# Attention: when the value products of a head pair are issued, and which engine copies the transposed scores out of PSUM

## The chip, the cores and the metric
One core of a Trainium2 chip. A time is device microseconds (us) of one execution; the kernel before takes 1093.11 us, the median of three runs (1092.77 to 1093.15).

## The reference
Rotary attention, and behind it two feed-forward layers on its output:

```
q, k, v: 4 x 8 heads x 576 x 64
scores = (1/8) * rotate(q) @ rotate(k)^T;  scores -= max over the keys
attn   = exp(scores) / (sum + 1e-9);       out = attn @ v
x = out as 2304 tokens x 512
x = elu(x @ w_in) @ w_out          (512 -> 2048 -> 512)
x = h - tanh(h), h = x @ w_in2;  x @ w_out2
```

## The kernel before
Attention works through 16 pairs of heads. One pair is nine steps: four blocks of 128 queries for each of the two heads (items 0 to 7, the heads alternating) and one item, 8, with the last 64 queries of both. Lines 402 to 436 write the order of the instructions out by hand, step by step over all pairs (i = 9 x pair + item), so every engine takes its work in exactly this order. Step i issues:

- VectorE: the row maximum of item i (L241, tile nm).
- TensorE: the scores of item i+1 (L232, tile s). There are two PSUM buffers for s, so these scores can only be written when the exponential of item i-1 has read its buffer.
- ScalarE: the exponential of item i out of PSUM into tile a (L255), with the row sums.
- flush (L282): the copies (evacuations) out of PSUM of what step i-1 transposed. The tile aT takes 128x512 elements of each item, aTr 128x128 for each second item and for item 8. A running counter ev shares the copies out: two of five go to VectorE (L286), three of five to ScalarE (L288). They are 14 in a pair, so which copy falls to which engine repeats after five pairs. After them flush copies finished outputs o to xa on ScalarE (L293).
- VectorE adds 1e-9 and takes the reciprocal of the row sums for items that are complete (L268, L269), and GpSimd (POOL) scales a by it (L272).
- A piece of the next pair's rotation (GpSimd L148, VectorE L150 and L157, ScalarE L153; from it q and k are put in place by DMAs on SP's queue, L194 and L197), and in some steps a piece of a feed-forward weight's conversion (L74 to L92).
- TensorE: the transposes of item i-4 (four into pt, L312; for each second item one more into pr, L322, and for item 8 L316). There are three PSUM buffers for pt and pr.
- TensorE: the value products that are due (L345, tile o). They come in visits. A group of queries (items 0 to 3; items 4 to 7; item 8) has five chunks of keys; for each chunk there is one product for each head, which stands in the trace as two instructions. Here the stationary matrix is 128 x 64, where scores and transposes use 128 x 128 (the form column says 128*64 and 128*128).

PV_AT (L401) gives for each group and chunk how many steps after the group's last transpose it is issued. Before the change a pair p has four visits: at step 8 of pair p three chunks of the first group (12 instructions); at step 1 of pair p+1 its other two (8); at step 3 three chunks of the second group (12); at step 5 its other two and the last group (28). The visit at a distance of 1 step reads aT tiles whose copies stand in the flush of the same step, behind that step's exponential.

The first pair's scores come out of a shorter path. After attention the first feed-forward layer (L472, L529) and the second (L758, L723) follow.

Of the kernel before, what the change touches and what calls it, by code (L numbers as in the profile page):

```python
# [23 lines left out]
def attention_elu_tanhshrink(ctx: ExitStack, tc: tile.TileContext, qk, v, w1i, w1o, w2i, w2o, tab, out):  # L24
# [35 lines left out]
    def load_w(key, eng=nc.sync):  # L60
        l, kind, c = key
        t = fm[:, 1024 * (nraw[0] % 2):1024 * (nraw[0] % 2) + 1024]
        nraw[0] += 1
        eng.dma_start(out=t.bitcast(mybir.dt.int64), in_=w_src[l, kind][c])
        raw_t[key] = t
# [43 lines left out]
    with ExitStack() as actx:  # L109
# [20 lines left out]
        def load_qk(p, x):  # L130
            t = p2.tile([128, 2, S], F32, tag=f"t{x}", name=f"t{x}")
            nc.sync.dma_start(out=t, in_=qk[p, :, 2 * x:2 * x + 2, :])
            t_t[p, x] = t

        def load_v(p):
            t = v_t[p] = vt_t[p % 2]
            nc.sync.dma_start(out=t[:, 0:512], in_=v[p, :, 0:512])
            for h in range(2):
                sl = slice(64 * h, 64 * h + 64)
                nc.sync.dma_start(out=t[sl, 512 + 64 * h:576 + 64 * h], in_=v[p, sl, 512:576])  # L140
            nc.sync.dma_start(out=t[64:128, 640:704], in_=v[p, 0:64, 512:576])
# [25 lines left out]
        def rotate_first(x):  # L167
            t = t_t.pop((0, x))
            prod = ps_s.tile([128, 2, 512], F32, tag="s", name="prod")[:, :, 0:288]
            for i in range(2):  # L170
                yield
                nc.vector.scalar_tensor_tensor(
                    out=two(t[:, 1, :]) if i else prod, in0=two(t[:, i, :]), scalar=(1.0 if x else SCALE),
                    in1=two(tabs[:, i, :]), op0=ALU.mult, op1=ALU.mult,
                )
            yield
            if x:
                nc.vector.tensor_tensor(out=two(rk), in0=prod, in1=two(t[:, 1, :]), op=ALU.add)
            else:
                for h in range(2):  # L180
                    sl = slice(64 * h, 64 * h + 64)
                    nc.vector.tensor_tensor(
                        out=two(rq[:, h, :])[sl], in0=prod[sl], in1=two(t[:, 1, :])[sl], op=ALU.add
                    )
            yield
# [53 lines left out]
        def emit_max(i):  # L239
            nm = sm.tile([128, 1], F32, tag="nm", name="nm")  # L240
            nc.vector.tensor_reduce(out=nm, in_=s_t[i][:, :, 0:288], axis=AX.XY, op=ALU.max, negate=True)  # L241
            nm_t[i] = nm

        def emit_exp(i):
            p, u, h = items[i]
            s = s_t.pop(i)
            if h in (0, None):
                if u < 4:
                    a_t[p, u] = p3.tile([128, 2, S], F32, tag="a", name="a")
                else:  # L250
                    a_t[p, u] = p1.tile([128, 1, S], F32, tag="a2", name="a2")
                n_t[p, u] = sm.tile([128, 2], F32, tag="den", name="den")
            a = a_t[p, u][:, h or 0, :]
            den = n_t[p, u][:, (h or 0):(h or 0) + 1]
            nc.scalar.activation(  # L255
                out=a.rearrange("p (x c) -> p x c", x=2), in_=s[:, :, 0:288], func=AF.Exp,
                bias=nm_t.pop(i), scale=1.0, accum_out=den,
            )

        def emit_norm(i):  # L260
            p, u, h = items[i]
            if h == 0:
                return
            nh = 2 if h == 1 else 1
            den = n_t.pop((p, u))[:, 0:nh]
            r = sm.tile([128, 2], F32, tag="r", name="r")
            for x in range(nh):
                nc.vector.tensor_scalar_add(den[:, x:x + 1], den[:, x:x + 1], 1e-9)  # L268
            nc.vector.reciprocal(out=r[:, 0:nh], in_=den)  # L269
            for x in range(nh):  # L270
                a = a_t[p, u][:, x, :]
                nc.gpsimd.tensor_scalar(  # L272
                    out=a, in0=a, scalar1=r[:, x:x + 1], scalar2=1.0, op0=ALU.mult, op1=ALU.mult
                )

        ev = [0]
# [5 lines left out]
        def flush():  # L282
            for out_, in_ in late:
                ev[0] += 1
                if ev[0] % 5 in (1, 3):
                    nc.vector.tensor_copy(out_, in_)  # L286
                else:
                    nc.scalar.copy(out_, in_)  # L288
            late.clear()
            for p, grp, o, n in late_x:  # L290
                b, hp = divmod(p, 4)
                x0 = NTOK * hp + b * S + 256 * grp
                nc.scalar.copy(out=xa[:, x0:x0 + n], in_=o[:, 0:n])  # L293
            late_x.clear()
# [75 lines left out]
        with tc.manual_schedule():  # L370
            for x in range(2):
                t_t[0, x] = p2.tile([128, 2, S], F32, tag=f"t{x}", name=f"t{x}")
            for i in range(2):
                nc.sync.dma_start(out=t_t[0, 1][:, i, :], in_=qk[0, :, 2 + i, :])
                nc.sync.dma_start(out=tabs[:, i, :], in_=tab[:, i, :])
                nc.sync.dma_start(out=t_t[0, 0][:, i, :], in_=qk[0, :, i, :])
            load_qk(1, 1)
            load_qk(1, 0)
            nc.vector.memset(xa[:, 0:512], 0.0)
            nc.vector.memset(zero, 0.0)  # L380
            nc.gpsimd.memset(rq[64:128, 0, :], 0.0)
            nc.gpsimd.memset(rq[0:64, 1, :], 0.0)
            make_identity(nc, ident)
            warm = ps_t.tile([128, 512], F32, tag="pt", name="warm")
            for i in range(8):
                nc.tensor.matmul(out=warm, lhsT=xa[:, 0:128], rhs=xa[:, 0:512], start=True, stop=True)
            for i in range(2):
                nc.scalar.copy(out=qa_t[i][:, S:640], in_=zero)
                nc.scalar.copy(out=qb_t[i][:, 0:64], in_=zero)
                nc.gpsimd.memset(vt_t[i][64:128, 512:576], 0.0)  # L390
                nc.gpsimd.memset(vt_t[i][0:64, 576:704], 0.0)
            rot = [rotate_first(1), rotate_first(0)]
            for i in range(4):
                for r in rot:
                    next(r)
            n = len(items)
            pend = []
            nw = list(range(len(first_w)))[::-1]
            emit_s(0)
            load_v(0)  # L400
            PV_AT = ((1, 1, 1, 3, 3), (1, 1, 1, 3, 3), (2, 2, 2, 2, 2))  # L401
            for i in range(n + D + 1):
                p, r = divmod(i, NI)
                for f, *arg in sched.get(i, ()):
                    if f is not prep:
                        f(*arg)
                if i == 7 or i % (2 * NI) == 12:
                    load_w(first_w[nw.pop()]) if nw else None
                if i < n:
                    emit_max(i)  # L410
                if i + 1 < n:
                    emit_s(i + 1)
                if i < n:
                    emit_exp(i)
                flush()
                if 0 <= i - 1 < n:
                    emit_norm(i - 1)
                if p < NPAIR:
                    for f, *arg in sched.get(i, ()):
                        if f is prep:  # L420
                            f(*arg)
                    c = r if p == 1 else NI * (p % 2) + r - 3 if p else -1
                    if c >= 0 and c % 2 == 0 and c // 2 < NCV and p // 2 < len(first_w):
                        key = first_w[p // 2]
                        conv_w(key, c // 2, 512 * (p // 2 % 3))
                if 0 <= i - D < n:
                    emit_t(i - D)
                    pp, uu, hh = items[i - D]
                    if uu in (1, 3) and hh == 1 or uu == 4:
                        for c in range(5):  # L430
                            pend.append((i + PV_AT[uu // 2][c], pp, uu // 2, c))
                for x in [x for x in pend if x[0] <= i]:
                    emit_pv(*x[1:])
                    pend.remove(x)
                if n - 8 <= i < n and (i - n) % 2 == 0:
                    split_x(0, (i - n + 8) // 2)
            while pend:
                emit_pv(*pend.pop(0)[1:])
            flush()


# [519 lines left out]
```

## Time and profile before

| | |
|---|---|
| median of three runs | 1093.11 us |
| the profiled execution | 1093.27 us, of which the profile's span 1090.8 us |
| TensorE (PE) busy | 1066.9 us, 98% of the span |
| VectorE (DVE) busy | 753.3 us, 69% |
| ScalarE (ACT) busy | 723.1 us, 66% |
| GpSimd (POOL) busy | 696.5 us, 64% |
| TensorE clock granted | full throughout |

Attention takes the first 302 us of the span; pair p's visit at step 8 starts at about 47 us for pair 1 and 277 us for pair 14. PE's busy time counts overlapping instructions whole and is no measure of how well it is used; the order of the waits tells more. PEld are TensorE's weight loads, which run ahead of its products.

### The profile page before, as it was taken

How to read it: one execution, taken by the hardware profiler on the slowest of the kernel's cores; microseconds unless marked ns; L12 is line 12 of the kernel's file. 1: busy time of each engine (PE TensorE's matmuls, PEld its weight loads, DVE VectorE, ACT ScalarE, POOL GpSimd, SP SyncE). 2: the span in 40 equal slices, each digit the busy share in tenths (PEclk: the TensorE clock that was granted, in tenths of full speed). 3: DMA queues.
4: the chain of work that ended last, by engine and by line, in shares of the span. 5: the costliest groups of instructions: out<-in, count | busy, mean ns of one | idle time of the engine just before them, and what ended most of it. 6: DMA issues, size and time to landing. Idle time of an engine off the chain costs nothing.

```text
span 1090.8 us, 18762 instructions
## 1 busy us (share of the span) xinstructions
PE 1066.9 (98%) x6480; PEld 959.0 (88%) x6480; DVE 753.3 (69%) x1436; ACT 723.1 (66%) x1560; POOL 696.5 (64%) x653
## 2 busy tenths in 40 slices
PE   8999999999999999999999999999999999999998
PEld 4777777777799999999999999988998999889986
DVE  7898888888546456675675665376766667766674
ACT  3677677777668656555555555588777877878762
POOL 5887888887568755555555556566567555755552
PEclk9999999999999999999999999999999999999999
DMA  7878777776224344354344672265545664556531
GB/s 237 224 185 214 178 206 195 206 199 173 59 69 143 129 153 136 117 164 166 115 145 139 216 260 81 94 224 202 175 163 176 248 212 175 176 167 221 172 126 58
DMA packets 86590, 182.75 MB, mean 168 GB/s; under 512 B 11745, under 2 KB 47585, under 8 KB 86497
## 3 DMA queue, kind: packets, MB, share of 16 engines
q1 hardware_dynamic: 78720, 153.25, 44.7%
q10 hardware_dynamic: 7776, 28.32, 8.7%
q8 instruction: 51, 0.84, 0.3%
q14 instruction: 43, 0.34, 0.1%
HBM read 127.21 MB, written 27.79 MB: 142 GB/s over the span
## 4 chain that ended last, share of the span: by engine, by line
PE 76%; DVE 11%; POOL 4%; ACT 3%; DMA 3%; issue 2%; SPq 0%; ACTq 0%; DVEq 0%; POOLq 0%
PE y L529 18%; PE h L472 18%; PE yb L723 14%; PE hb L758 9%; PE o L345 6%; PE s L232 5%; PE cvb L758 3%; PE pt L312 3%; DVE nm L241 3%; DVE aT L286 1%; DVE fn L791 1%; DMA qb<-hl 1%; ACT a L255 1%; POOL blk L513 1%; DVE t L150 1%
## 5 line engine op out<-in xcount | busy, mean ns | idle before, releaser
L513 POOL TENSOR_TENSOR gt<-fn,gt 128x384 fp32r<-128x384 f32 x119 | 123.1, 1035 | 78.2 <-ACT gt L512 66.2
L272 POOL TENSOR_SCALAR a<-a,r 128x576 f32<-128x576 f32 x144 | 138.4, 973 | 48.2 <-DVE r L269 31.1
L255 ACT ACTIVATE a<-s,nm 128x576 f32<-128x576 f32 x144 | 107.0, 743 | 90.7 <-DVE nm L241 76.0
L723 PE MATMUL yb<-wb,blk 128*128 128x512 f32 x603 | 154.3, 392 | 0.4 <-POOL blk L513 0.4
L758 PE MATMUL hb<-blk,wa 128*128 128x384 f32 x720 | 139.9, 337 | 2.0 <-DVE fn L791 2.0
L758 PEld LDWEIGHTS hb<-blk,wa 128*128 128x128 f32 x720 | 127.1, 188 | 7.3 <-DVE fn L791 3.0
L723 PEld LDWEIGHTS yb<-wb,blk 128*128 128x128 f32 x603 | 112.5, 188 | 22.6 <-POOL blk L513 0.8
L480 ACT ACTIVATE fn<-h 128x384 f32<-128x384 f32 x96 | 47.3, 493 | 128.4 <-PE h L472 109.6
L241 DVE TENSOR_REDUCE nm<-s 128x1 f32<-128x576 f32 x144 | 107.9, 752 | 28.3 <-PE s L232 25.1
L513 POOL TENSOR_TENSOR blk<-fn,blk 128x384 fp32r<-128x384 f32 x67 | 71.1, 1061 | 87.9 <-ACT blk L512 59.6
L472 PE MATMUL h<-blk,wa 128*128 128x384 f32 x576 | 107.8, 335 | 0.8 <-POOL blk L55 0.6
L529 PE MATMUL y<-gt,wa 128*128 128x384 f32 x576 | 107.7, 334 | 0.1
L529 PE MATMUL y<-gt,wb 128*128 128x384 f32 x576 | 107.5, 334 | 0.0
L472 PE MATMUL h<-blk,wb 128*128 128x384 f32 x576 | 107.5, 334 | 0.0
L497 DVE TENSOR_SCALAR cvb<-fm 128x512 f32<-128x512 f32 x56 | 38.9, 694 | 98.1 <-ACT fm L495 95.7
L472 PEld LDWEIGHTS h<-blk,wa 128*128 128x128 f32 x576 | 100.3, 188 | 1.8 <-POOL blk L55 0.9
L529 PEld LDWEIGHTS y<-gt,wa 128*128 128x128 f32 x576 | 100.5, 188 | 0.4 <-issue 0.4
L529 PEld LDWEIGHTS y<-gt,wb 128*128 128x128 f32 x576 | 100.5, 188 | 0.0
L472 PEld LDWEIGHTS h<-blk,wb 128*128 128x128 f32 x576 | 100.5, 188 | 0.0
L92 POOL TENSOR_TENSOR fm<-fm,fn 128x512 fp32r<-128x512 f32 (+1 forms) x48 | 58.3, 1218 | 55.8 <-ACT fn L91 52.5
L345 PE MATMUL o<-aT,v 128*64 128x256 f32 (+1 forms) x768 | 89.5, 336 | 3.2 <-ACT aT L288 2.8
L148 POOL TENSOR_TENSOR t<-t,tabs 128x576 f32<-128x576 f32 x58 | 82.9, 1430 | 7.2 <-DMA t<-in_qk 7.2
(136 smaller groups left out, 2290.3 us busy)
## 6 DMA issues: line engine op xcount, KB each, us to landing
wa<-wi SPq DMA_DIRECT2D x96, 448.0 KB, 4.9
wb<-wo SPq DMA_DIRECT2D x48, 512.0 KB, 6.4
t<-in_qk SPq DMA_DIRECT2D x30, 576.0 KB, 5.1
k<-hl SPq DMA_DIRECT2D x60, 288.0 KB, 4.4
fm<-in_w2o ACTq DMA_DIRECT2D x16, 512.0 KB, 3.6
fm<-in_w2i ACTq DMA_DIRECT2D x14, 512.0 KB, 3.7
fm<-in_w1i ACTq DMA_DIRECT2D x12, 512.0 KB, 3.7
wi<-fn SPq DMA_DIRECT2D x24, 256.0 KB, 2.2
```

What stands on the lines that cost most here:

```text
L92: nc.gpsimd.tensor_tensor(out=lo, in0=f, in1=hi.bitcast(F32), op=ALU.subtract)
L148: eng.tensor_tensor(out=t[:, i, :], in0=t[:, i, :], in1=tabs[:, i, :], op=ALU.mult)
L232: nc.tensor.matmul(out=s[:, half, o0:o0 + n], lhsT=w, rhs=k[:, part, c0:c0 + n], start=(m == 0 and part == 0), stop=(m == len(terms) - 1 a ...
L241: nc.vector.tensor_reduce(out=nm, in_=s_t[i][:, :, 0:288], axis=AX.XY, op=ALU.max, negate=True)
L255: nc.scalar.activation(out=a.rearrange("p (x c) -> p x c", x=2), in_=s[:, :, 0:288], func=AF.Exp, bias=nm_t.pop(i), scale=1.0, accum_out=den,)
L272: nc.gpsimd.tensor_scalar(out=a, in0=a, scalar1=r[:, x:x + 1], scalar2=1.0, op0=ALU.mult, op1=ALU.mult)
L345: nc.tensor.matmul(out=o[sl, 0:n], lhsT=w, rhs=m, start=(c == 0), stop=(c == 4))
L472: nc.tensor.matmul(out=hp, lhsT=w[:, wp, ws], rhs=x_hl(t, xp, c), start=(m == 0), stop=(m == 3 * KC - 1))
L513: nc.gpsimd.tensor_tensor(out=g[:, 1, :], in0=f, in1=g[:, 0, :].bitcast(F32), op=ALU.subtract)
L529: nc.tensor.matmul(out=y_t[e][:, 0:NB], lhsT=w[:, wp, es], rhs=gt[:, gp, :], start=st, stop=sp)
L723: nc.tensor.matmul(out=y, lhsT=gt[:, gp, es], rhs=w[:, wp, :], start=(j == 0 and k == 0), stop=(j == NJ - 1 and k == 2))
L758: nc.tensor.matmul(out=bank, lhsT=w[:, wp, o:o + 128], rhs=x[:, xp, cc, :], start=(start and k == 0), stop=(stop and k == 5), skip_group_c ...
```

## The change
The first group's five chunks are all issued two steps after its last transpose, that is at step 0 of the next pair (20 instructions), instead of three at step 8 and two at step 1. A pair then has three visits, at steps 0, 3 and 5 of the next pair. The second and third group keep their places. And VectorE takes one copy in five where it took two: the copies whose counter is 3 modulo 5 go to ScalarE.

```diff
         def flush():
             for out_, in_ in late:
                 ev[0] += 1
-                if ev[0] % 5 in (1, 3):
+                if ev[0] % 5 == 1:
                     nc.vector.tensor_copy(out_, in_)
                 else:
                     nc.scalar.copy(out_, in_)
...
-            PV_AT = ((1, 1, 1, 3, 3), (1, 1, 1, 3, 3), (2, 2, 2, 2, 2))
+            PV_AT = ((2, 2, 2, 2, 2), (1, 1, 1, 3, 3), (2, 2, 2, 2, 2))
```

## Rows read from the trace of the kernel before

**Rows 1.** Chain of waits from 38 to 303 us, shares by line
```profile
by line: PE o L345 24.1%; PE s L232 19.7%; PE pt L312 11.8%; DVE nm L241 10.2%; DVE aT L286 4.3%; ACT a L255 3.2%; DVE t L150 2.8%; DMA qb<-hl 2.7%; DMA v<-in_v 2.6%; ACT aT L288 2.5%; issue 2.5%; DMA k<-hl 2.0%; DVE hl L157 1.7%; POOL a L2
```

**Rows 2.** Chain around 31, 212, 243 and 323 us: start, us, what
```profile
31.19 7.16 DMA qb<-hl
...
40.39 5.28 DMA k<-hl
...
211.54 1.01 PE o L345 x8
212.55 0.73 PE s L232 x4
...
213.83 0.54 PE s L232 x4
...
215.06 1.45 PE o L345 x12
216.50 0.73 PE s L232 x4
...
322.68 2.08 PE y L529 x12
```

**Rows 3.** Busy time of each engine over ten pairs, sum; and one pair
```profile
206.68:224.44 17.76, 17.30 (x144) 13.57 (x143) 16.41 (x34) 12.37 (x34) 16.44 (x16) 1.00 0.74 203
...
sum 176.39, PE 171.74 PEld 135.63 DVE 153.47 ACT 125.30 POOL 145.39; mean PE 17.17 PEld 13.56 DVE 15.35 ACT 12.53 POOL 14.54
```

**Rows 4.** Waits from 38 to 302 us: us in total, times, longest
```profile
ACT a L255 <- DVE nm L241: 60.9, 63, 2.0
...
PEld o L345 <- ACT aT L288: 8.3, 14, 1.0
...
PEld s L232 <- ACT a L255: 4.5, 11, 0.8
...
PEld pr L316 <- ACT aT L288: 4.2, 3, 1.6
```

**Rows 5.** Timeline of PE: first group's visits at step 8, start and duration
```profile
82.54 2.21 PE L345 MATMUL o<-aT,v 128*64 128x256 f32 x12
...
154.64 1.51 PE L345 MATMUL o<-aT,v 128*64 128x256 f32 x12
...
206.68 0.65 PE L345 MATMUL o<-aT,v 128*64 128x256 f32 x2
207.78 1.51 PE L345 MATMUL o<-aT,v 128*64 128x256 f32 x10 [0.46 <-ACT aT L288]
```

**Rows 6.** Timeline: step 8's transposes and exponential, pairs 6 and 12
```profile
136.07 0.60 PE L312 MATMUL pt<-ident,a 128*128 128x128 f32 x4
136.43 0.74 ACT L255 ACTIVATE a<-s,nm 128x576 f32<-128x576 f32 x1 [0.47 <-DVE nm L241]
...
241.38 0.60 PE L312 MATMUL pt<-ident,a 128*128 128x128 f32 x4
241.55 0.74 ACT L255 ACTIVATE a<-s,nm 128x576 f32<-128x576 f32 x1
```

**Rows 7.** Copies on VectorE (L286) and ScalarE (L288): ns min/median/max
```profile
L286 DVE COPY aT<-pt x58: 673/681/691, 21.6 to 299.8; 128x512 f32<-128x512 f32 x58
L286 DVE COPY aTr<-pr x32: 275/281/283, 23.5 to 293.1; 128x128 f32<-128x128 f32 x32
...
L288 ACT COPY aT<-pt x86: 574/576/631, 24.4 to 297.6; 128x512 f32<-128x512 f32 x86
L288 ACT COPY aTr<-pr x48: 254/272/333, 33.0 to 300.0; 128x128 f32<-128x128 f32 x48
```

**Rows 8.** Timeline: second group's visit at step 3, pairs 1, 3 and 12
```profile
54.79 2.14 PE L345 MATMUL o<-aT,v 128*64 128x256 f32 x12
...
90.18 0.14 PEld L316 LDWEIGHTS pr<-ident,a 128*128 128x128 f32 x1 [0.17 <-DVE aT L286]
...
250.43 0.33 PE L316 MATMUL pr<-ident,a 128*128 128x128 f32 x1 [1.33 <-ACT aT L288]
```

## The prediction

> **What bounds the kernel now.** I read the chain of waits first. From about 314 us on it is products of the feed-forward layers, one after another without a gap: twelve in 2.08 us, and again twelve [rows 2]. Nothing the change touches lies there, so what attention gains or loses arrives at the end one for one. Up to 46 us the chain runs through DMAs that put q and k of pair 1 in place (7.16 and 5.28 us [rows 2]); time that TensorE saves in pair 0 is hidden behind them. What counts are pairs 1 to 15.
>
> From 38 to 303 us the chain [rows 1] is on TensorE for somewhat over half (o 24.1, s 19.7, pt 11.8%), and most of the rest is on VectorE (maxima 10.2, copies aT 4.3, rotation 2.8 and 1.7%); ScalarE's exponentials and copies have 3.2 and 2.5%. So TensorE sets the pace, but it stops often, and the stops are then followed back through ScalarE to VectorE. The busy times of ten pairs say the same [rows 3]: 176.39 us, 17.64 for a pair, of which VectorE is busy 15.35, POOL 14.54, ScalarE 12.53. VectorE is the fullest of the three that feed TensorE. The list of waits closes the ring [rows 4]: ScalarE's exponentials wait 60.9 us for VectorE's maximum, while the value products' weight loads wait 8.3 us for ScalarE's copies of aT, pr of item 8 4.2 us for such a copy, and the scores 4.5 us for an exponential that frees their buffer.
>
> **The change part by part.** I work against the profiled execution, 1093.27 us, 0.16 us above the median of the runs.
>
> *One visit less.* Twelve instructions of o take 1.45 us and eight 1.01 [rows 2], so one is (1.45 - 1.01) / 4 = 0.11 and the merged twenty take 1.45 + 8 x 0.11 = 2.33 instead of 2.46: 0.13 less, the price of going in. The scores right behind a visit take 0.73 us, those behind a transpose 0.54 [rows 2], so coming out costs 0.19 or 0.20. Together 0.33 us for a visit; in 15 pairs **-5.0 us**. Bounds: nothing, where TensorE then waits for something else anyway, and these 5.0.
>
> *The stall at step 8 goes.* Twelve instructions with nothing to wait for take 1.51 us in the timeline (154.64, pair 7). In pair 3 they take 2.21; in pair 10 two of them start at 206.68 and the other ten end at 207.78 + 1.51 = 209.29, 2.61 in all [rows 5]. The first two read head 0, whose copy came a step earlier; the ten stand behind the copy of item 3, which ScalarE makes in this very step after its exponential. Of pairs 1 to 14, eight show this stall (1, 3, 5, 6, 8, 10, 11, 13), those in which item 3's copy is on ScalarE; added up over 1.51 each they lose 6.9 us. One step later these copies have long been made: **-6.9 us**.
>
> *What is late next.* Without the visit, the instruction behind step 8's transposes is step 0's score (item 1 of the next pair), and that needs the buffer which step 8's exponential reads. Today the visit covers this. In pair 6 the transposes start at 136.07 and take 0.44 in the chain, so TensorE would be ready at 136.51, but the exponential ends at 136.43 + 0.74 = 137.17: a wait of 0.66. In pair 12 it is 242.29 against 241.82, 0.47 [rows 6]. Of pairs 6 to 12 I read six this way; they give 0.66, 0.34, 0.55, 0.58, 0.09 and 0.47, mean 0.45. Queued behind the waiting score on TensorE are step 0's transposes, the twenty products and step 1's score, and for the score waits VectorE's next maximum. The trace of before cannot show the wait itself; it lies between nothing (the exponential comes earlier than today) and 0.66 a pair (9.2 us in 14). I take the mean of the readings, 14 x 0.45 = **+6.3 us**. So the stall that goes is largely exchanged for another; pairs without a stall today (7, 9, 12) gain little.
>
> *45 copies from VectorE to ScalarE.* VectorE makes 58 + 32 copies, and the counter gives half of them away: 29 x 0.681 + 16 x 0.281 = 24.2 us less on VectorE, and 29 x 0.576 + 16 x 0.272 = 21.1 us more on ScalarE [rows 7]. Per pair VectorE goes from 15.35 to 13.9 us busy and ScalarE from 12.53 to 13.9, both of some 17. ScalarE's room for it is the time in which it waits for the maximum, 60.9 us [rows 4]; without that cover the 21.1 would lie on the path. What VectorE's relief is worth: its aT copies hold 4.3% of the 265 us of the chain [rows 1], 11.4 us, and half of them go, so at most 5.7 us; at least less than nothing, since a copy that is in the way on ScalarE takes 0.576 too. I take half the upper end, **-2.9 us**, because the maxima that ScalarE waits for stand behind these copies, while ScalarE's own share of the chain is small.
>
> The Trainium skill, page TensorEngine Tiling (Array Packing), section PSUM Bottleneck, says that after TensorE is sped up the copies out of PSUM may become the bound, and to use both engines for them. By that rule moving copies onto one engine is a step in the wrong direction and the last term would have the other sign; by the rows above ScalarE is the emptier of the two. What it would do here is the rival on the slow side below.
>
> *Item 7's copy.* It is read one step after, as before, by the visit at step 3. With period five in the pairs: it stays on VectorE in pairs 0, 5, 10, stays on ScalarE in 1, 2, 4 and moves to ScalarE in 3, 8, 13. In pair 3, on VectorE, the weight load of item 8's pr waits 0.17 us; in pair 1 the visit takes 2.14 for 1.51, and in pair 12 pr waits 1.33 for ScalarE [rows 8]. Three pairs gain a stall (0.7 each, pair 1's stall with the pr behind it), three in which pr's buffer would now be freed on ScalarE gain 0.2 each, and in pairs 2, 7, 12 VectorE is quicker to the maximum (I take back 0.5 each): 2.1 + 0.6 - 1.5 = **+1.2 us**, between -1.5 and 6 x 1.33 = 8.0.
>
> Sum: -5.0 - 6.9 + 6.3 - 2.9 + 1.2 = -7.3 us. 1093.27 - 7.3 = 1086.0 us for an execution like the profiled one, 1085.8 as a median.
>
> **The rivals.**
>
> *More: the new wait does not come.* If VectorE's relief brings step 8's exponential forward by half a microsecond, the score finds its buffer free and the +6.3 falls away: -13.6, 1079.5 us. For it: in that stretch VectorE is often the chain. Against: in pair 12 the exponential waits for nothing that the profile names and still ends 0.47 late.
>
> *Nothing: TensorE was not the bound.* Between the visits at step 5 and step 0 lie steps 6, 7 and 8 without products. TensorE has about 3.9 us of scores and transposes there, while VectorE has three maxima, the rotation and its share of the conversion. If TensorE simply runs up against the two score buffers in each pair, every saving becomes a wait: the 5.0 and 2.9 are lost, and what remains, -6.9 + 6.3 + 1.2, leaves 1093.7 us (within 0.2%). For it: VectorE busy 16.41 of 17.76 us in a pair with conversion [rows 3]. Against: the same change takes 1.5 us a pair off VectorE. POOL, 16.44 in that pair, cannot become much shorter either, but 14.54 on the mean leaves room.
>
> *Slower: ScalarE's queue becomes the path.* ScalarE takes its work in order, so each copy that is added stands ahead of the next exponential, and the exponential ahead of a score buffer. The place is steps 6 to 8, where TensorE now has no products to fill the time. If 0.576 + 0.272 are added to step 8's exponential in each pair, the wait there is 0.45 + 0.85 = 1.3 us, +18.2 in 14 pairs instead of +6.3, and item 7's copies cost 8.0 instead of 1.2: -5.0 - 6.9 + 18.2 + 8.0 = +14.3 without the relief, 1107 us; with the relief taken above, 1104. It decides from the point where ScalarE's copies end later than the maximum that the next exponential needs. Against it: 60.9 us of waiting for maxima. The skill's rule above points this way.
>
> That the change does not do what it says I can exclude from the code: both edits alter which instructions stand where.
>
> **How the numbers follow.** Forecast (-3 to -12 us) 0.57; more than that 0.19; nothing 0.13; slower 0.11. Faster or slower by over 0.2% (2.2 us, about what can be told from no change here): faster 0.57 + 0.19 = 0.76, same 0.13, slower 0.11. The range takes in the forecast's own, the greater part of the case of more, down to 1078 us, and the half of the case of nothing, up to 1091.5 us; about 2 in 10 stay outside.
>
> **What would show it.** In the changed trace: three visits a pair, of 20, 12 and 28 instructions, the twenty in some 2.33 us without a wait for aT; the scores behind step 8's transposes waiting some 0.3 to 0.6 us for an exponential (a wait of scores for ScalarE of 8 to 11 us instead of 4.5); 45 copies fewer on VectorE; ScalarE waiting clearly less than 60.9 us for maxima; the stall at item 8's pr in three pairs more. The pair's period would be 17.1 to 17.3 us. The forecast is wrong if the scores' wait is near nothing (then more is gained), or if the chain goes through ScalarE's copies into exponentials.

## The result

The changed kernel takes 1104.76 us (median of four runs, 1104.03 to 1105.62) where the kernel before takes 1093.13 on the same chip: 11.6 us slower, ratio 1.0106 with a 95% interval of 1.0089 to 1.0124. I had forecast 1085.8 us. The profiled execution took 1105.62 us, its span 1103.6.

Busy time of each engine on the page of the changed kernel:

```profile
PE 1063.0 (96%) x6480; PEld 959.1 (87%) x6480; DVE 736.3 (67%) x1391; ACT 740.7 (67%) x1605; POOL 695.3 (63%) x653
```

VectorE lost its 45 copies and ScalarE gained them, as meant. The feed-forward layers are not touched: the last short products of o begin at 315.09 us instead of 302.12, so the whole loss arises in attention.

Waits of the changed kernel from 38 to 315 us (engine and line, what it waited for: us in total, times, longest):

```profile
DVE nm L241 <- PE s L232: 47.2, 49, 2.8
ACT a L255 <- DVE nm L241: 46.1, 55, 2.3
...
ACT a L255 <- DVE den L268: 21.8, 27, 1.4
PEld s L232 <- ACT a L255: 20.0, 34, 2.0
PEld pr L316 <- ACT aT L288: 11.2, 9, 1.7
...
PE pr L316 <- ACT aT L288: 9.1, 9, 1.4
PE s L232 <- ACT a L255: 8.9, 22, 1.7
...
PE s L232 <- DMA v<-in_v: 2.7, 5, 0.8
...
PEld o L345 <- ACT aT L288: 1.9, 3, 0.7
```

And two lines of the kernel before (38 to 302 us) to set beside them:

```profile
DVE nm L241 <- PE s L232: 23.8, 38, 2.3
...
ACT a L255 <- DVE den L268: 10.1, 13, 1.4
```

Against [rows 4]: the value products hardly wait for copies any more (1.9 us for 8.3). In exchange the scores' weight loads wait 20.0 us for an exponential to free their buffer (4.5 before), item 8's pr waits nine times instead of three, and at the top stands a wait that I had not thought of: VectorE's maxima wait 47.2 us for scores, in the kernel before 23.8. The engine that I had called the fullest is standing idle.

Two of these rows need care. The exponentials of the rows "<- DVE den" do not read what that addition writes; in the timeline they start about 0.1 us after their maximum ends, and the addition only ends in between. With these rows counted in, ScalarE waits 67.9 us for maxima (46.1 + 21.8) instead of 71.0 (60.9 + 10.1), hardly less. And VectorE's idle time is no price by itself: in e2_share below, where VectorE has only lost copies, its maxima wait 43.1 us, and the kernel is 3.8 us slower.

One pair shows how. Timeline of PE in the changed kernel, from pair 2's step 8 on (start, duration, what; in brackets the idle time before it and what ended it):

```profile
64.31 0.60 PE L312 MATMUL pt<-ident,a 128*128 128x128 f32 x4
65.53 0.77 PE L232 MATMUL s<-k,qb 128*128 128x288 f32 x4 [0.62 <-DMA v<-in_v]
...
66.77 1.95 PE L345 MATMUL o<-aT,v 128*64 128x256 f32 x16
68.55 0.60 PE L345 MATMUL o<-aTr,v 128*64 128x256 f32 x4
69.08 0.80 PE L232 MATMUL s<-k,qa 128*128 128x288 f32 x4
...
70.68 0.60 PE L312 MATMUL pt<-ident,a 128*128 128x128 f32 x4
71.12 0.27 PE L322 MATMUL pr<-ident,a 128*128 128x128 f32 x1
71.65 0.80 PE L232 MATMUL s<-k,qa 128*128 128x288 f32 x4 [0.26 <-ACT a L255]
72.29 0.60 PE L312 MATMUL pt<-ident,a 128*128 128x128 f32 x4
73.86 0.33 PE L316 MATMUL pr<-ident,a 128*128 128x128 f32 x1 [0.97 <-ACT aT L288]
```

And the chain of waits of the same kernel over the second half of that stretch (start, us, what):

```profile
66.84 2.31 PE o L345 x20
69.15 0.74 PE s L232 x4
69.89 0.02 issue
69.92 0.76 DVE nm L241
70.67 0.07 DVE den L268
70.75 0.02 issue
70.77 0.83 ACT a L255 x2
71.60 0.48 ACT aT L288
...
73.86 0.33 PE pr L316
```

There are three stops. Step 0's score starts at 65.53; the transposes ahead of it were through at 64.31 + 0.44 = 64.75, so 0.78 us are lost: the stop that I forecast. The twenty instructions then take 2.31 us in one go (forecast 2.33). While they run VectorE and ScalarE work off the two score buffers and fall idle. Behind them everything starts anew from one score: maximum at 69.92, exponential, copy. TensorE meets that chain twice: at step 3's score (71.65, where the transposes ahead were through at 70.68 + 0.44 + 0.11 = 71.23: 0.42 lost), and at pr of item 8, which needs the buffer of item 7's copy (ready at 72.29 + 0.44 = 72.73, started at 73.86, 1.13 lost). The chain shows that this part is no longer TensorE's own pace, but the restart of the pipeline behind a long visit.

Counted the same way from the PE timeline, over what follows step 8 of pairs 1 to 14, step 0's score loses 11.4 us, step 3's score 5.8 (0.41 or 0.42 each time) and item 8's pr 11.0 (nearly all of it in nine pairs). In the kernel before, step 0's score stands right behind a visit and step 3's loses nothing; pr loses 4.3.

### The profile page after: what moved, and what is told of

Read it like the earlier page. It is cut to its first block, busy times and chain, and to the rows that moved or that the text cites. A ratio compares the mean times of both kernels' runs of the same rounds, so it can differ in the third digit from the quotient of the medians.

```text
span 1103.6 us, 18769 instructions
## 1 busy us (share of the span) xinstructions
PE 1063.0 (96%) x6480; PEld 959.1 (87%) x6480; DVE 736.3 (67%) x1391; ACT 740.7 (67%) x1605; POOL 695.3 (63%) x653
## 4 chain that ended last, share of the span: by engine, by line
PE 75%; DVE 10%; ACT 5%; POOL 5%; DMA 3%; issue 3%; SPq 0%; ACTq 0%; DVEq 0%; POOLq 0%
PE y L529 18%; PE h L472 18%; PE yb L723 14%; PE hb L758 9%; PE o L345 6%; PE s L232 4%; PE cvb L758 3%; DVE nm L241 3%; PE pt L312 2%; DMA v<-in_v 2%; ACT a L255 1%; DVE t L150 1%; DMA k<-hl 1%; PE warm L386 1%; DVE fn L791 1%
## 5 line engine op out<-in xcount | busy, mean ns | idle before, releaser
L92 POOL TENSOR_TENSOR fm<-fm,fn 128x512 fp32r<-128x512 f32 (+1 forms) x48 | 58.2, 1217 | 53.4 <-ACT fn L91 52.1
L312 PE MATMUL pt<-ident,a 128*128 128x128 f32 x576 | 87.0, 274 | 0.1
L148 POOL TENSOR_TENSOR t<-t,tabs 128x576 f32<-128x576 f32 x58 | 82.4, 1422 | 6.8 <-DMA t<-in_qk 6.7
```

Source lines behind the costliest of these rows:

```text
L92: nc.gpsimd.tensor_tensor(out=lo, in0=f, in1=hi.bitcast(F32), op=ALU.subtract)
L148: eng.tensor_tensor(out=t[:, i, :], in0=t[:, i, :], in1=tabs[:, i, :], op=ALU.mult)
L312: nc.tensor.transpose(pt[:, c, :], a[:, h or 0, c0:c0 + 128], ident)
```

## The experiments

Edits are against the kernel before, if nothing else is said. Theory A was that the merged visit by its place and length makes the time; theory B that ScalarE's queue does, because of the copies.

**Each half of the change alone.** e1_place has the visits only (the second line of the diff), e2_share the copies only (the first).

```diff
-            PV_AT = ((1, 1, 1, 3, 3), (1, 1, 1, 3, 3), (2, 2, 2, 2, 2))
+            PV_AT = ((2, 2, 2, 2, 2), (1, 1, 1, 3, 3), (2, 2, 2, 2, 2))
```

> The visits of the change alone; VectorE keeps two copies in five. Theory A (the place and length of the merged visit make the time: it uncovers the score of step 0, which waits for step 8's exponential, and starves VectorE for 2.3 us, after which scores and item 7's copy come late): 1099 to 1107 us. Theory B (ScalarE's queue is the path, because of the 45 copies): 1084 to 1092 us, since the copies have not moved.

> The copies of the change alone; the visits stay as they were. Theory A: 1088 to 1096 us, hardly any difference. Theory B: 1099 to 1105 us.

e1_place: 1107.42 us, ratio 1.0138 (1.0121 to 1.0155), 14.4 us slower. e2_share: 1096.77 us, ratio 1.0032 (1.0019 to 1.0045), 3.8 us slower. Theory B falls: without one copy moved the loss is there, and larger. On top of the new visits the moved copies may help a little (the changed kernel's 1.0106 stands against 1.0138), but the two intervals touch, and the profiled executions took the same time (1105.62 and 1105.36 us).

In e2_share VectorE's maxima wait nearly as long for scores as in the changed kernel (waits from 38 to 316 us):

```profile
DVE nm L241 <- PE s L232: 43.1, 75, 2.5
```

**The place and the joining apart.** e3_merge8 puts all twenty instructions at step 8, e5_split01 moves them one step later but keeps two visits, e8_five makes three of them.

```diff
-            PV_AT = ((1, 1, 1, 3, 3), ...
+            PV_AT = ((1, 1, 1, 1, 1), ...      e3_merge8
+            PV_AT = ((2, 2, 2, 3, 3), ...      e5_split01
+            PV_AT = ((1, 1, 2, 2, 3), ...      e8_five
```

> The first group's five chunks in one visit at step 8 (distance 1 for all), the copies two in five. Theory A1 (what costs is that steps 6 to 8 and 0 have no visit that covers the score of step 0): 1086 to 1093 us, since step 8 is covered again. Theory A2 (what costs is the length: twenty instructions in one go starve VectorE wherever they stand): 1098 to 1106 us. Theory B: 1086 to 1092 us.

> The first group's products all later than before, but in two visits: three chunks at step 0 and two at step 1 (distances 2, 2, 2, 3, 3); copies two in five, as in the kernel before. If the length of one go of twenty is what costs: 1091 to 1097 us, most of the 14 us of the merged visit come back. If the empty step 8 is what costs, whatever stands at steps 0 and 1: 1101 to 1108 us.

> One visit more instead of one less: the first group's chunks at distances 1, 1, 2, 2, 3 (steps 8, 0, 1; 8, 8 and 4 instructions); copies two in five. If each visit is worth 0.33 us on the path: 1097 to 1099 us. If an evener spread feeds VectorE better than that costs: 1086 to 1092 us.

e3_merge8: 1101.49 us, ratio 1.0082 (1.0067 to 1.0097). e5_split01: 1095.40 us, ratio 1.0022 (1.0012 to 1.0031). e8_five: 1099.82 us, ratio 1.0063 (1.0048 to 1.0078). So the place costs little (2.8 us in e5); joining at one place or the other costs most (8.5 us in e3; from e5's 2.8 to 14.4 in e1). And a visit more costs 7.2 us, 0.48 for each of 15 pairs, somewhat more than I expected. That fits a price of a visit on the path, 0.33 by my rows, but the spacing changes too, so e8 does not show the price alone. Waits of e1_place and then of e5_split01, from 38 to 316 us, same columns as above:

```profile
ACT a L255 <- DVE nm L241: 62.4, 67, 2.0
DVE nm L241 <- PE s L232: 37.1, 32, 2.8
```

```profile
ACT a L255 <- DVE nm L241: 57.5, 64, 2.0
DVE nm L241 <- PE s L232: 30.4, 42, 2.2
```

With VectorE's work unchanged its idle time before maxima is 23.8 us in the kernel before, 30.4 in e5 and 37.1 in e1, that is 6.6 and 13.3 more, beside 2.8 and 14.4 us of time. This does not show the cause: an engine with the same work is idle longer whenever the same work takes longer.

The PE timelines show more, counted over pairs 1 to 14 as above. Step 0's score loses 11.9 us in e5 and 11.9 in e1, so joining is not paid there. Step 3's score loses nothing in e5 and 6.1 in e1, and item 8's pr 3.2 and 6.7: joining is paid behind step 1, which has a visit in e5 and none in e1.

**Is it k's DMA?** In five pairs the profile names a DMA as what released step 0's score (the row "<- DMA v<-in_v" above, a load that no score reads; the DMAs that put k in place are issued on the same queue). e4_k_early is the changed kernel with k's rotation one step earlier.

```diff
-   ((-10, -6, -4, -3, -2, -1), (-7, -2, 0, 2, 3, 4))[x]
+   ((-10, -6, -4, -3, -2, -1), (-7, -3, -1, 1, 2, 3))[x]
```

> The change as it is, with k's rotation (its last four pieces) one step earlier, so that k's DMAs to their place start one step sooner. If the score of step 0 waits for the landing of k, as the trace's releaser says in five pairs: 1099 to 1102 us. If it waits for step 8's exponential all the same: 1104 to 1106 us.

1104.86 us, ratio 1.0110 (1.0095 to 1.0125), what the changed kernel has. In its timeline of PE the same score (s from qb at step 0) still waits, now for the exponential everywhere, and for less time: counted as above it loses 7.5 us over 14 pairs instead of 11.4. Three of them:

```profile
214.68 0.80 PE L232 MATMUL s<-k,qb 128*128 128x288 f32 x4 [0.50 <-ACT a L255]
...
232.70 0.80 PE L232 MATMUL s<-k,qb 128*128 128x288 f32 x4 [0.56 <-ACT a L255]
...
251.54 0.80 PE L232 MATMUL s<-k,qb 128*128 128x288 f32 x4 [0.55 <-ACT a L255]
```

The landing of the DMA fell close to the end of the exponential or somewhat behind it. That the 3.9 us do not show in the kernel's time says that the landing is not what makes it slow.

**Length or missing cover?** Two kernels leave out two of the first group's five chunks; e13_short_one does the other three in one visit at step 0, e14_short_two in two visits as before.

```diff
-                        for c in range(5):
+                        for c in ((0, 1, 4) if uu < 2 else range(5)):
```

> Leaves out two of the first group's five chunks (8 of its 20 instructions); the other three in one visit at step 0, as in the change; copies two in five. To be set against e14_short_two, which does the same work in two visits. If the joined visit costs by its length, 12 instructions are no longer than the other visits and it is at most 3 us slower than e14, or faster by up to 5. If the missing cover at step 1 is what costs: 8 to 14 us slower than e14.

> Leaves out the same two chunks; two chunks at step 8 and the last at step 1, as in the kernel before; copies two in five. If TensorE's time in products is on the path as it stands, 16 x 8 x 0.11 = 14 us less than the kernel before, 1079 us; if VectorE is what bounds, 1087 to 1093 us.

e13: 1094.80 us, ratio 1.0016 (1.0006 to 1.0025); e14: 1087.67 us, ratio 0.9948 (0.9933 to 0.9963). The short joined visit still costs 7.1 us against the split one, the long one 14.4. Neither theory alone holds: about half stays when the joined visit is no longer than others, and goes with the visit that is missing where the scores need cover; the other half, by difference, goes with the length. The PE timelines bear the first half out: step 3's score, counted as above, loses 5.6 us in e13 and 0.1 in e14. Besides, e14 takes 16 x 8 x 0.11 = 14 us of products away from TensorE and gains only 5.3. So in the kernel before, the products left out are on the path for little more than a third of their time.

**Who is on the path?** e9_noadd and e10_after_noadd leave out the additions of 1e-9 to the row sums (144 short instructions of VectorE), in the kernel before and in the changed one.

```diff
-            for x in range(nh):
-                nc.vector.tensor_scalar_add(den[:, x:x + 1], den[:, x:x + 1], 1e-9)
```

> The kernel before without the additions of 1e-9 to the row sums (144 instructions of VectorE, 0.07 to 0.14 us each; left out of the computation, and a row sum that is at least 1 stays the same). If VectorE is what bounds attention, so that its idle time is what the merged visit costs: 5 to 10 us less, 1083 to 1088 us. If TensorE is bound by its own order and the two score buffers: 1090 to 1093 us.

> The changed kernel without the same additions. VectorE is less loaded here and idles more behind the merged visit. If the merged visit costs because VectorE's restart after it is a chain (maximum, sums, rotation, maximum, exponential, copy): 4 to 10 us less than the changed kernel, 1095 to 1101 us. If its cost lies only in TensorE's order: 1103 to 1105 us.

e9: 1089.60 us, ratio 0.9963 (0.9949 to 0.9977), 3.5 us less: between the two expectations. e10: 1100.34 us, ratio 1.0063 (1.0048 to 1.0078), 4.4 us less than the changed kernel. Easing VectorE helps both, but not by the 17.1 us of its busy time that went in e9 (753.3 to 736.2 us); it is one link of a ring, no more the sole bound than TensorE is.

**Which copy is on which engine.** e6_h1 keeps the old visits and gives VectorE the aT copy of each item of the second head (1, 3, 5, 7), ScalarE all others. e7_h1_place adds the change's visits to it. e12_keep7 has the change's copies, but item 7's stays with the engine it had (the third argument of evac is called keep there).

```diff
-        def evac(out_, in_):
-            late.append((out_, in_))
+        def evac(out_, in_, dve=False):
+            late.append((out_, in_, dve))
...
-                if ev[0] % 5 in (1, 3):
+                if dve:                                              e6, e7
+                if ev[0] % 5 == 1 or keep and ev[0] % 5 == 3:        e12
...
-            evac(aT[:, h, :, q0:q0 + 128], pt)
+            evac(aT[:, h, :, q0:q0 + 128], pt, h == 1)               e6, e7
+            evac(aT[:, h, :, q0:q0 + 128], pt, u == 3 and h == 1)    e12
```

> Visits as in the kernel before; VectorE copies the aT tile of each item of the second head (items 1, 3, 5, 7: four of 14) right behind its maximum, ScalarE all others. The copies that the visits at distance 1 read no longer stand behind an exponential. If those visits' stalls (6.9 us at step 8 and about as much at step 3 in the kernel before) are really on the path: 1080 to 1088 us. If they only take the place of waits that come anyway: 1091 to 1096 us.

> The same copies as in the run before this one, with the visits of the change. If the place of the merged visit costs by itself, whoever makes the copies: 10 to 15 us above that run. If it cost only together with late copies of item 7: at most 3 us above it.

> The copies of the change (one in five on VectorE), visits as before, but the copy of item 7 stays with the engine that had it in the kernel before. If the 3.8 us that the copies alone cost are the three pairs in which item 7's copy moves behind an exponential: 1091 to 1094 us. If they are ScalarE's load in general: 1095 to 1098 us.

e6: 1086.98 us, ratio 0.9947 (0.9932 to 0.9962), 5.6 us faster than the kernel before. e7: 1101.21 us, 14.2 us above e6; the merged visit costs the same whoever makes the copies. e12: 1093.74 us, ratio 1.0009 (0.9999 to 1.0018): of the 3.8 us that the copies alone cost, 3.1 are item 7's (2.5 by the ratios). The waits of e2_share and then of e12_keep7 (38 to 316 us) carry it:

```profile
PEld pr L316 <- ACT aT L288: 8.9, 9, 1.3
```

```profile
PEld pr L316 <- ACT aT L288: 5.8, 6, 1.0
```

The waits of e6_h1 show VectorE idle less than in the kernel before (18.1 us for 23.8), and no line in which pr or the products wait for a copy of aT is among its eleven longest:

```profile
ACT a L255 <- DVE nm L241: 47.4, 53, 1.5
...
DVE nm L241 <- PE s L232: 18.1, 31, 1.6
```

VectorE also has less to copy in e6 (64 copies of aT, 43.4 us, instead of 58 and 32 of aTr, 48.3 us). That is not the gain: in e12 it is relieved of 22 us of copies and nothing is gained.

**A version that beats both.** e11_h1_noadd is e6 without the additions, which the reference has; e15_h1_oneadd is e6 with one addition for both columns, which leaves nothing out.

```diff
-            for x in range(nh):
-                nc.vector.tensor_scalar_add(den[:, x:x + 1], den[:, x:x + 1], 1e-9)
+            nc.vector.tensor_scalar_add(den, den, 1e-9)              e15
```

> VectorE copies aT of the second head, ScalarE all else, the visits as in the kernel before, and no additions of 1e-9. If the two gains are of different waits: 1078 to 1083 us. If they are of the same waits: 1084 to 1087 us, no better than the copies alone.

> The whole computation: VectorE copies aT of the second head, ScalarE all else, the visits as in the kernel before, and one addition of 1e-9 to both columns of the row sums instead of two (64 instructions of VectorE fewer). Of the 6.1 us that leaving out all 144 additions gave on these copies about 64/144 or a little more: 1083 to 1085 us; if the additions mattered by the waits that they carry, not by their number: 1085 to 1087 us.

e11: 1080.90 us, ratio 0.9883 (0.9868 to 0.9897). e15: 1086.79 us, ratio 0.9944 (0.9927 to 0.9961). So the fastest takes 12.2 us less than the kernel before and 24 less than the changed one. The gains of e6 (5.6) and e9 (3.5) add up, and somewhat more. That 64 instructions fewer gain nothing beside e6, and the 80 others 5.9 us, is no matter of their number: the joined additions take longer. The additions of e6 and then of e15 (ns min/median/max), and one joined addition in e15's timeline:

```profile
L268 DVE TENSOR_SCALAR den<-den x144: 135/142/154, 16.4 to 289.0; 128x1 f32<-128x1 f32 x144
```

```profile
L267 DVE TENSOR_SCALAR den<-den x80: 134/226/1467, 16.4 to 288.6; 128x2 f32<-128x2 f32 x64, 128x1 f32<-128x1 f32 x16
```

```profile
50.75 1.47 DVE L267 TENSOR_SCALAR den<-den 128x2 f32<-128x2 f32 x1
50.78 1.41 POOL L148 TENSOR_TENSOR t<-t,tabs 128x576 f32<-128x576 f32 x1
```

Summed up, the additions take 20.3 us in e6 and 32.4 in e15. Of the 64 joined ones 41 take more than 0.2 us, and each of these ends 0.02 to 0.03 us after a TENSOR_TENSOR of POOL ends (L148, L92 or L55). Of the one-column additions of e6, 62 start during such an instruction and still take 0.14 to 0.15 us. So a joined addition that meets such an instruction is held until that is through; why, no run here tells.

## Why the prediction was wrong

- *One visit less, -5.0 us.* The length was right: twenty instructions take 2.31 us against my 2.33. The Trainium skill, page TensorEngine Tiling (Array Packing), section Key Properties, says that a change of tiling mode drains TensorE; the rows agree that going in and out takes time (0.13 and 0.19 to 0.20 us), and no run here shows whether a drain is the reason. But I took the saving as if TensorE's time were on the path throughout; by e14 only 5.3 of 14 us were.
- *The stall at step 8 goes, -6.9 us.* It went: in the changed kernel's timeline the twenty instructions take 2.31 us in every pair, without a stall. e6 shows that these stalls and those at step 3 were worth 5.6 us together when they are taken away without moving a visit, less than the some 15 us that they sum up to (6.9 at step 8; 4.0 of the products and 4.3 of pr at step 3), since other waits follow.
- *What is late next, +6.3 us.* This is the step that failed. I looked at the first instruction behind the place that the visit left (step 0's score) and took 0.45 us a pair, at most 9.2 in all; it loses 11.4, so even there the upper bound was too low. I did not ask the same of the other place that lost its visit, step 1: the score of step 3, which I put at nothing, loses 5.8 us. In e5, which keeps a visit at step 1, it loses nothing. Nor did I ask what the engines behind TensorE do while twenty instructions run: behind them, as the chain shows, maximum, exponential and copy start anew from one score, and item 7's copy comes late.
- *45 copies, -2.9 us.* Wrong in sign with the old visits (e2: +3.8); on top of the merged visit the medians differ by 2.8 (11.6 for 14.4 us), but that is hardly clear of the noise, so it does not confirm the term. The place of the copy decides, not the load: 3.1 of the 3.8 us are item 7's. The relief of VectorE's, which I had valued, became idle time: its maxima wait 43.1 us for scores in e2.
- *Item 7's copy, +1.2 us.* Right in kind, too small: 3.1 us alone (e2 less e12), and beside the merged visit pr loses 11.0 us instead of 4.3. The waits went from three to nine pairs: new are 3, 8 and 13, which I had named, and 4, 9 and 14, where pr now waits 1.43, 1.44 and 0.75 us by the timeline and I had taken 0.2 each.
- *The sum.* Put with what the timeline shows, the waits are 11.4 + 5.8 + (11.0 - 4.3) = 23.9 us more, where I had 6.3 + 1.2 = 7.5. Less the 6.9 of old stalls at step 8 and the 5.0 for the visit that makes 12.0 us, near the 11.6 measured, with nothing left for the relief of VectorE. It is an estimate from one execution of each kernel.
- *The rivals.* The case of nothing, that TensorE runs up against the two score buffers between visits, was the right mechanism; I priced it as a saving that is lost and not as a loss, since I let it end at the first wait and did not follow it to the next steps. The slow case, 1104 us, came near the measured time by another cause: e1 is slow with no copy moved.
- *The range* ended at 1091.5 us because the bounds of the new wait were taken from one step of the pair.

What stays open: how the cost of joining divides between length and cover beyond the halves of e13 and e14, and why a joined addition is held by POOL.

## What to carry to other kernels

Before joining two pieces of work to save the switch between them, look at each place that loses a piece as the cover of what follows, and ask at every one of them what the next instruction will then wait for, up to the point where the order of before is back. An engine's idle time is no measure of what this costs: here VectorE waited nearly as long for scores with 3.8 us lost (e2) as with 11.6. Where a copy is read one step after, give it to the engine whose queue does not hold it behind that step's longest instruction; which copy goes where was worth 5.6 us here, how many of them 0.7 (e12), which is not clear of the noise.

## What I had not expected of the hardware

A wait that the profile puts down to a DMA (0.76 us at one pair's step 0 score in the changed kernel) vanished as a DMA and stayed as a wait for the exponential, 0.56 us, when the DMAs of k came earlier (e4): of several things that a score waits for, the row names only the last to come. And one addition of two columns on VectorE took up to 1.47 us, until an instruction of POOL was through, where an addition of one column took at most 0.15 us at the same places (e15 and e6): joining two short instructions made 12 us of work more, and the kernel no faster (1086.98 and 1086.79 us).
